# Projections in front of the down stage, softmax differences kept in PSUM, and layer norms finished by fours

## The chip, the cores and the metric

The kernel runs on one core of a Trainium2 chip. The metric is device time in microseconds, from the start to the end of one execution. An execution that was recorded by the hardware profiler gives the trace; its own time stands beside its span below.

## The reference

```python
xn = layernorm(x)                         # x: 2048 rows of 640
q, k, v = split(xn @ wqkv)                # 32 heads of 20
# row s attends to the 8 rows s, s-2, ..., s-14 (masked below row 0)
logits = einsum("bhsd,bhswd->bhsw", q, kg) * scale
o = einsum("bhsw,bhswd->bhsd", softmax(logits), vg)
h = (xn_B @ w_gate) * (xn_B @ w_up)       # 640 -> 1536; xn_B is the same xn
out = x + o @ wo + h @ w_down
```

Inputs and output are bf16.

## The kernel before

The 2048 rows are 16 tiles of 128 rows (t), four to a chunk (c = 0 to 3, `CH = 4`). For each chunk there are these stages:

- **Norm** (`ln`): for tiles 8 to 15 ScalarE takes the negative mean (`ln_mean`, L312) and the sum of squares (`ln_square`, L319), each with an accumulator output of one column; GpSimd makes three operations of one column per tile (L325, L327, L348); ScalarE applies the result to x in place (L355). Tiles 0 to 7 are done on VectorE.
- **Transposes** (`transposes`): from tile 4 on a transposing DMA on the SP queue (L395) writes xnT of the chunk, which has `XB` buffers.
- **Projections** (`project`, `proj`, L502 and L506): q, k and v, five groups of five matmuls each, each group evicted by ScalarE. `halo` copies the last 14 columns of the chunk before (L449). q, k and v have two buffers each, so chunk c + 2 writes over chunk c.
- **Products and logits** (`products`, `fold`, L565, L536, L541): VectorE multiplies q with shifted k and folds the result; `logits` (L587) sums over the head's dimensions with TensorE, into a bank of its own with two buffers.
- **Softmax** (`softmax`), twice per chunk (n = 0 to 7): maximum (L615), difference (L619), exp on ScalarE (L628), sum (L635), reciprocal (L638), scaling (L642) on VectorE; then the weights are stored to DRAM (aD, L648) and spread back over the partitions (aE, L654), both on the SP queue.
- **Weighted values** (`av`): per tile two products of v and aE (L681) and a tree of three additions (L691, L689) that ends in oT.
- **Gate and up** (`glu`): 24 groups of matmuls (L714), evicted by ScalarE (L719) into gs and us, and multiplied on VectorE into hT (L731); hT has 12 buffers, one chunk's.
- **Down** (`down`): per tile the matmuls of hT with wd (L780) and of oT with wo (L783), evicted to y (L795) and added to the output by a GpSimd DMA (L824); the last two tiles are added on VectorE (L791) and stored by SP.

Every operation is a `Step` with an engine, a cost, a part of the cost that occupies the engine (`occ`), and the steps it depends on. `Plan.order` simulates the engines with these costs, and at each time gives a free engine the ready step with the smallest latest time (`late`). The order that comes out is the program order of each engine's queue; on the chip each engine works its queue strictly in that order. All matmul groups but the logits are one chain in the order of declaration (`pe_main`), with a ring of six PSUM banks for their results. `margin` adds time, in the plan alone, after the steps that a step waits for. A transfer with `kb` ends in the plan by this rule, where its cost counts for `late` alone:

```python
if s.kb:
    s.end = queue[s.eng] = max(t0 + 2.0, queue.get(s.eng, 0.0)) + s.kb / 340
```

TensorE's chain is: projections of chunks 0 and 1, gate and up 0, down 0, projections 2, gate and up 1, down 1, projections 3, gate and up 2, down 2, gate and up 3, down 3. The norms of tiles 8 to 15 may start, by `LN_HOLD`, after hT products 2 to 5 of chunks 0 and 1.

Of the kernel before, what the change touches and what calls it, by code (L numbers as in the profile page):

```python
# [9 lines left out]
ACT = mybir.ActivationFunctionType  # L10
# [101 lines left out]
def kernel(  # L112
# [57 lines left out]
    def new(key, shape, dtype, tag, bufs, pool=None):  # L170
        t = (pool or sb).tile(shape, dtype, name=tag, tag=tag, bufs=bufs)
        T[key] = t
        return t
# [122 lines left out]
    def apply_in(t):  # L296
        XT[t] = inline("DVE", 0.443, ln_apply(t), [RS[t]], 0.4)

    LN_ACT = 8

    ST_ACT = (8, 9, 10, 11, 12, 13, 14, 15)

    LN_HOLD = ((0,2),(0,3),(0,4),(0,5),(1,2),(1,3),(1,4),(1,5))

    def held(at):
        return HT[at] if len(at) == 2 else R[at[0], at[1]][at[2]]

    def ln_mean(t):
        def fn():
            sq = new(("sq", t), [P, D], BF, "sq", 1)  # L310
            nm = new(("nm", t), [P, 1], F32, "nm", 6)
            nc.scalar.activation(sq[:], T["x", t][:], ACT.Identity, scale=-1.0 / D, accum_out=nm[:])  # L312
        return fn

    def ln_square(t):
        def fn():
            sq = new(("sq", t), [P, D], BF, "sq", 1)
            ss = new(("ss", t), [P, 1], F32, "ss", 4)
            nc.scalar.activation(sq[:], T["x", t][:], ACT.Square, bias=T["nm", t][:], accum_out=ss[:])  # L319
        return fn  # L320

    def ln_rstd_sq(t):
        def fn():
            ve = new(("ve", t), [P, 1], F32, "ve", 6)
            nc.gpsimd.tensor_scalar(ve[:], T["ss", t][:], scalar1=1.0 / D, scalar2=EPS, op0=ALU.mult, op1=ALU.add)  # L325
            rs = new(("rstd", t), [P, 1], F32, "rstd", 6)
            nc.gpsimd.tensor_tensor(rs[:], ve[:], mhalf[:], ALU.pow)  # L327
        return fn

    def ln(t):  # L330
        turn = [XT.get(t - (1 if t == CH else 2)), GL.get(t - 1)] if t < 2 * CH else []
        if t in ST_ACT:
            a = GL[t] = add("ACT", 0.95, ln_mean(t), [X[t], held(LN_HOLD[t - 2 * CH])], occ=0.87)
            a = add("ACT", 1.05, ln_square(t), [a], occ=0.97)
            b = RS[t] = add("POOL", 1.6, ln_rstd_sq(t), [a])
        else:
            a = add("DVE", 0.48, ln_stats(t, 0), [X[t], GL.get(t - 3), *turn], occ=0.395)
            a = add("DVE", 0.48, ln_stats(t, 1), [a], occ=0.395)
            a = GL[t] = add("DVE", 0.39, ln_aggr(t), [a], occ=0.3)
            b = RS[t] = add("POOL", 0.56, ln_rstd(t), [a])  # L340
        if t < LN_ACT:
            XT[t] = add("DVE", 0.443, ln_apply(t), [b], occ=0.35)
            return

        if t in ST_ACT:
            def shift():
                ns = new(("ns", t), [P, 1], F32, "ns", 6)
                nc.gpsimd.tensor_tensor(ns[:], T["nm", t][:], T["rstd", t][:], ALU.mult)  # L348
        else:
          def shift():  # L350
              ns = new(("ns", t), [P, 1], F32, "ns", 6)
              nc.gpsimd.tensor_scalar(ns[:], T["mv", t][:, 0:1], scalar1=T["rstd", t][:], scalar2=-1.0, op0=ALU.mult, op1=ALU.mult)

        def apply():
            nc.scalar.activation(T["x", t][:], T["x", t][:], ACT.Identity, scale=T["rstd", t][:], bias=T["ns", t][:])  # L355

        b = add("POOL", 0.5, shift, [b])
        XT[t] = add("ACT", 0.95, apply, [b], occ=0.85)


    ring = []
# [8 lines left out]
        return main  # L370

    XDMA = 4
    EARLY = False
    XB = 3 if EARLY else 2
    GP = {}

# [200 lines left out]
    def logits(c, g):  # L577
        n = 2 * c + g

        def lg():  # L580
            l = new(("lps", n), [P, W, E], F32, "pl", 2, psum)
            parts = [summed(c, 2 * g + b) for b in range(2)]
            last = len(parts[0]) - 1
            for i in range(last + 1):
                for b in range(2):
                    for j in range(4):
                        nc.tensor.matmul(l[H * j : H * (j + 1), 4 * b : 4 * b + 4, :], lhsT=Ek[:],  # L587
                                         rhs=parts[b][i][:, :, E * j : E * (j + 1)],
                                         start=(i == 0 and b == 0), stop=(i == last), tile_position=(0, H * j), skip_group_check=True)

        alone = not (g and c in PAIRED)
        took = 0.022 + 0.2195 * (len(LEFT) if c == 0 else 1) + (0.19 if alone else 0.0)
        LL[n] = add("PE", took + 0.13, lg, [FO[2 * n], FO[2 * n + 1], FO[4 * c + 3] if c in PAIRED else None, LL.get(n - 1), DD.get(n - 2), CE], occ=took)
        LL[n].urgent = True
        LL[n].margin = (0.9 if c == 0 else 3) if alone else 0.0

# [6 lines left out]
    def softmax(c, hf):  # L603
        n = 2 * c + hf

        def small(op, occ, deps):
            return add("DVE", occ + 0.083, op, deps, occ=occ)

        def mask():
            ps = T["lps", n]  # L610
            nc.vector.tensor_tensor(ps[0:H, :, 0:HALO], ps[0:H, :, 0:HALO], negm[0:H], ALU.add)

        def top():
            m = new(("m", n), [P, E], F32, "m", 1)
            nc.vector.tensor_reduce(m[:], T["lps", n][:].rearrange("p w s -> p s w"), AX.X, ALU.max)  # L615

        def sub():
            d = new(("d", n), [P, W, E], F32, "d", 1)
            nc.vector.tensor_tensor(d[:], T["lps", n][:], T["m", n][:, None, :].to_broadcast([P, W, E]), ALU.subtract)  # L619

        a = LL[n]
        if n == 0:
            a = small(mask, 0.2, [a, CM])
        a = small(top, 0.6, [a])
        DD[n] = small(sub, 0.609, [a, AA.get(n - 1)])

        def ex():
            nc.scalar.activation(T["d", n][:], T["d", n][:], ACT.Exp, scale=scale)  # L628

        e = add("ACT", 0.635, ex, [DD[n]], occ=0.54)  # L630
        e.margin = 0.8

        def total():
            s = new(("s", n), [P, E], F32, "s", 1)
            nc.vector.tensor_reduce(s[:], T["d", n][:].rearrange("p w s -> p s w"), AX.X, ALU.add)  # L635

        def rec():
            nc.vector.reciprocal(T["s", n][:], T["s", n][:])  # L638

        def scaled():  # L640
            a = new(("a", n), [P, W, E], BF, "a", 1)
            nc.vector.tensor_tensor(a[:], T["d", n][:], T["s", n][:, None, :].to_broadcast([P, W, E]), ALU.mult)  # L642

        AA[n] = small(scaled, 0.609, [small(rec, 0.47, [small(total, 0.6, [e])]), AS.get(n - 1)])

        def store():
            aD = new(("aD", n), [H, 4, W * E], BF, "aD", 2, dram)
            nc.sync.dma_start(out=aD[:].rearrange("h e f -> e h f"), in_=T["a", n][:].rearrange("p w s -> p (w s)"))  # L648

        def spread():  # L650
            ae = new(("aE", n), [P, 4, W, E], BF, "aE", 2)
            src = T["aD", n][:]
            src = bass.AP(tensor=src.tensor, offset=src.offset, ap=[[4 * W * E, H], [0, JL], [1, 4 * W * E]])
            nc.sync.dma_start(out=ae[:], in_=src)  # L654

        AS[n] = add("SP", 2.4, store, [AA[n], AE.get(n - 2)], occ=0.5, kb=128)
        AE[n] = add("SP", 3.5, spread, [AS[n], AM.get(2 * n - 3)], occ=0.5, kb=512)

    AS = {}
    ONE = True  # L660

# [6 lines left out]
    def av(t):  # L668
# [25 lines left out]
        w = LL[1] if t < 2 else O16.get(t - 2)  # L694
        a = add("DVE", 1.48, mul(0), [AE[n], w, *R[2, c]], occ=1.40, after=[O16.get(t - 1) if ONE else AM.get(t - 1)])
        a = AM[t] = add("DVE", 1.48, mul(1), [AE[n]], occ=1.40, after=[a])
        b = add("DVE", 1.485, tree(4), [a], occ=1.4)
        b = add("DVE", 0.82, tree(2), [b], occ=0.74)
        O16[t] = OE[t] = add("DVE", 0.49, tree(1), [b, DT.get(t - 4)], occ=0.41)

# [179 lines left out]
    proj(0, 1)  # L880
    proj(0, 2)

    def between(c, work):
        for q in range(CH):
            work(q)
            if c < NCH:
                ln(c * CH + q)
                transposes(c * CH + q)

    def attention(c):  # L890
        prodlog(c)
        if c == 0:
# [16 lines left out]
    for c in range(NCH):  # L909
        attention(c)  # L910
        glu(c)
        if c == 0:
            GS[0] = CM
            seed(0)
        for n in range(1, NCH):
            if SEED_AT[n][0] == c:
                seed(n)
        if EARLY:
            if c + 2 < NCH:
                for t in range((c + 2) * CH, (c + 3) * CH):  # L920
                    ln(t)
                    transposes(t)
                project(c + 2)
            for q in range(CH):
                down(c * CH + q)
        else:
            between(c + 2, lambda q: down(c * CH + q))
            if c + 2 < NCH:
                project(c + 2)

    for s in plan.order():
        s.fn()
# [30 lines left out]
```

## Time and profile before

| | us |
|---|---|
| median of 3 runs (260.49 to 261.25) | 261.0 |
| profiled execution, its own time | 260.88 |
| its span, first to last instruction | 259.2 |
| TensorE busy | 252.5 |
| VectorE busy | 228.6 |
| ScalarE busy | 128.8 |
| GpSimd busy | 47.9 |
| mean granted TensorE clock | 0.998 |

In the lines of the profile PE is TensorE, PEld its weight loads, DVE VectorE, ACT ScalarE, POOL GpSimd, SPq the SP queue. A line of a group has its line in the code, engine, operation, output and input, shape and count; behind the bar its busy time in us and the mean of one in ns; behind the second bar the engine's idle time just before these instructions and what ended it. A line of a timeline has the start and the duration in us, and in brackets the idle time before it.

### The profile page before, as it was taken

How to read it: one execution, taken by the hardware profiler on the slowest of the kernel's cores; microseconds unless marked ns; L12 is line 12 of the kernel's file. 1: busy time of each engine (PE TensorE's matmuls, PEld its weight loads, DVE VectorE, ACT ScalarE, POOL GpSimd, SP SyncE). 2: the span in 40 equal slices, each digit the busy share in tenths (PEclk: the TensorE clock that was granted, in tenths of full speed). 3: DMA queues.
4: the chain of work that ended last, by engine and by line, in shares of the span. 5: the costliest groups of instructions: out<-in, count | busy, mean ns of one | idle time of the engine just before them, and what ended most of it. 6: DMA issues, size and time to landing. Idle time of an engine off the chain costs nothing.

```text
span 259.2 us, 3845 instructions
## 1 busy us (share of the span) xinstructions
PE 252.5 (97%) x1493; PEld 140.2 (54%) x1493; DVE 228.6 (88%) x299; ACT 128.8 (50%) x251; POOL 47.9 (18%) x77
## 2 busy tenths in 40 slices
PE   7999999999999999999999999999999999999795
PEld 2955554444677554444476655444466744445562
DVE  5769999999999898999999967989999976999911
ACT  2756555699721365699931354555522242752100
POOL 2520000036641100036931200000302110000110
PEclk9999999999999999999999999999999999999999
DMA  7998996102274303015085241020112451020221
GB/s 223 333 206 236 397 374 229 58 3 101 57 147 43 34 6 97 0 23 182 3 183 73 25 85 41 16 88 0 51 52 25 41 75 64 0 101 3 25 25 53
DMA packets 19970, 24.49 MB, mean 94 GB/s; under 512 B 9104, under 2 KB 17296, under 8 KB 19888
## 3 DMA queue, kind: packets, MB, share of 16 engines
q1 hardware_dynamic: 16608, 17.70, 22.3%
q0 software_dynamic: 2384, 5.41, 12.8%
q10 hardware_dynamic: 960, 1.15, 1.2%
q8 instruction: 11, 0.18, 0.3%
q14 instruction: 7, 0.06, 0.1%
HBM read 18.61 MB, written 5.96 MB: 95 GB/s over the span
## 4 chain that ended last, share of the span: by engine, by line
DVE 41%; PE 39%; DMA 17%; issue 1%; ACT 0%; SPq 0%
PE ps L502 12%; PE ps L714 10%; DVE av L681 9%; PE ps L780 9%; DMA aE<-aD 9%; DVE pw L565 8%; DMA aD<-a 8%; DVE av L691 6%; DVE pw L536 4%; PE ps L783 4%; DVE hT L731 3%; PE ps L476 2%; DVE s L635 2%; PE ps L243 2%; DVE d L619 2%; DVE a L642 2%
## 5 line engine op out<-in xcount | busy, mean ns | idle before, releaser
L780 PE MATMUL ps<-wd,hT 128*128 128x320 bf16 (+2 forms) x384 | 57.8, 299 | 2.0 <-DVE hT L731 2.0
L714 PE MATMUL ps<-xnT,wg 128*128 128x512 bf16 x240 | 59.7, 379 | 0.0
L714 PE MATMUL ps<-xnT,wu 128*128 128x512 bf16 x240 | 59.6, 379 | 0.0
L681 DVE TENSOR_TENSOR av<-v,aE 128x2560 bf16<-128x2560 bf16 x32 | 47.1, 1486 | 10.2 <-DMA aE<-aD 10.2
L780 PEld LDWEIGHTS <-hT 128*128 128x128 bf16 x384 | 36.9, 98 | 18.6 <-DVE hT L731 2.6
L565 DVE TENSOR_TENSOR pw<-q,k 128x2560 bf16<-128x2560 bf16 x28 | 40.6, 1485 | 1.5 <-ACT k L506 1.5
L714 PEld LDWEIGHTS <-wu 128*128 128x128 bf16 x240 | 23.4, 98 | 28.3 <-issue 0.2
L714 PEld LDWEIGHTS <-wg 128*128 128x128 bf16 x240 | 23.3, 98 | 28.0 <-issue 0.4
L691 DVE TENSOR_TENSOR av<-av 128x2560 bf16<-128x2560 bf16 (+1 forms) x32 | 36.9, 1153 | 0.3
L719 ACT CAST gs<-ps 128x512 bf16<-128x512 f32 x48 | 28.1, 586 | 15.9 <-PE ps L714 15.8
L795 ACT COPY y<-ps 128x320 f32<-128x320 f32 x28 | 11.5, 427 | 49.0 <-PE ps L783 34.5
L719 ACT CAST us<-ps 128x512 bf16<-128x512 f32 x48 | 28.1, 584 | 13.8 <-PE ps L714 13.7
L824 POOL DMA_DIRECT2D out_dram<-y x14 | 12.2, 870 | 80.8 <-ACT y L795 78.3
L783 PE MATMUL ps<-wo,oT 128*128 128x320 bf16 (+2 forms) x160 | 27.0, 299 | 0.0
L536 DVE TENSOR_TENSOR pw<-pw 128x2048 bf16<-128x2048 bf16 (+1 forms) x28 | 25.1, 951 | 0.0
L502 PE MATMUL ps<-xnT,wk 128*128 128x512 bf16 x100 | 22.6, 380 | 0.0
L502 PE MATMUL ps<-xnT,wv 128*128 128x512 bf16 x100 | 22.2, 379 | 0.0
L731 DVE TENSOR_TENSOR hT<-gs,us 128x512 bf16<-128x512 bf16 x48 | 20.0, 417 | 0.4 <-ACT us L719 0.4
L325 POOL TENSOR_SCALAR ve<-ss 128x1 f32<-128x1 f32 x8 | 7.6, 952 | 66.1 <-ACT sq L319 65.7
L783 PEld LDWEIGHTS <-oT 128*128 128x128 bf16 x160 | 15.5, 98 | 6.3
L502 PEld LDWEIGHTS <-wv 128*128 128x128 bf16 x100 | 11.7, 117 | 9.8
L506 ACT CAST k<-ps 128x512 bf16<-128x512 f32 x20 | 11.7, 586 | 10.5 <-PE ps L502 10.5
(69 smaller groups left out, 224.0 us busy)
## 6 DMA issues: line engine op xcount, KB each, us to landing
aE<-aD SPq DMA_DIRECT2D x8, 512.0 KB, 3.6
out_dram<-y POOLq DMA_DIRECT2D x14, 160.0 KB, 3.7
out_dram<-in_A_x_dram POOLq DMA_DIRECT2D x3, 640.0 KB, 5.0
wg<-in_B_w_gate_dram SPq DMA_DIRECT2D x1, 1920.0 KB
wu<-in_B_w_up_dram SPq DMA_DIRECT2D x1, 1920.0 KB, 12.7
wd<-in_B_w_down_dram SPq DMA_DIRECT2D x1, 1920.0 KB
x<-in_A_x_dram SPq DMA_DIRECT2D x11, 160.0 KB, 6.1
aD<-a SPq DMA_DIRECT2D x8, 128.0 KB
```

The lines of the kernel that those rows point to most:

```text
L502: nc.tensor.matmul(T[key][:, 0:n], lhsT=lhs(r, i, j), rhs=T["xnT", c][:, i, lo : lo + n], start=(i == 0), stop=(i == KT - 1))
L506: nc.scalar.copy(where(r, c, j, j + 1, lo, n)[:, 0, :], T[key][:, 0:n])
L536: nc.vector.tensor_tensor(w[:, :, lo:hi, :], w[:, :, lo:hi, :], w[:, :, a:b, :], ALU.add)
L565: nc.vector.tensor_tensor(o, qh, kh, ALU.mult)
L681: nc.vector.tensor_tensor(o, v, w, ALU.mult)
L691: nc.vector.tensor_tensor(v[:, 0:k], v[:, 0:k], v[:, k : 2 * k], ALU.add)
L714: nc.tensor.matmul(ps[:], lhsT=(wu if r else wg)[:, i, f * P : (f + 1) * P], rhs=T["xnT", c][:, i, :], start=(i == 0), stop=(i == KT - 1))
L719: nc.scalar.copy(s[:], T[key][:])
L731: nc.vector.tensor_tensor(h[:], T["gs", c, f][:], T["us", c, f][:], ALU.mult)
L780: nc.tensor.matmul(ps, lhsT=T["hT", c, f][:, q * P : (q + 1) * P], rhs=wd[:, f, sl], start=(f == 0), stop=(f == FT - 1 and not wo_part))
L783: nc.tensor.matmul(ps, lhsT=T["oT", t][:, g, :], rhs=wo[:, g, sl], start=False, stop=(g == KT - 1 and f1 == FT))
L824: nc.gpsimd.dma_start(out=out_flat[t * P : (t + 1) * P, :], in_=T["y", t][:], accum_op=ALU.add)
```

## The change

- For chunks 2 and 3 the norms, transposes and projections are declared in front of the down stage of chunk 0 and 1 (`EARLY = True`), so TensorE's chain becomes: gate and up 0, projections 2, down 0, gate and up 1, projections 3, down 1, and on as before. xnT has three buffers instead of two.
- `ln_chunk` takes the place of `ln` for tiles 8 to 15. The means and sums of squares of four tiles go to four columns of one tile each; after the fourth, GpSimd makes three operations on four columns; then the four applies follow. `LN_HOLD` lets the norms of tiles 8 to 11 start after evictions of k and v of chunk 1, and those of 12 to 15 after the last hT product of chunk 0.
- The difference of the softmax is written over the logits in their PSUM bank, and exp, sum and scaling work there. The bank is free for logits n + 2 after the scaling instead of the difference.
- Costs in the plan: the store 3.3 instead of 2.4, the spread 3.9 instead of 3.5, the mask 0.18 instead of 0.2. `BY_DMA` is empty, so the tree of additions stays on VectorE.

```diff
-    LN_HOLD = ((0,2),(0,3),(0,4),(0,5),(1,2),(1,3),(1,4),(1,5))
+    LN_HOLD = ((1,1,0),(2,1,0),(2,1,2),(2,1,4),(0,11),(0,11),(0,11),(0,11))
...
+    def ln_finish(c):
+        def fn():
+            n4 = [P, CH]
+            ve = new(("ve4", c), n4, F32, "ve4", 2)
+            nc.gpsimd.tensor_scalar(ve[:], T["ss", c][:], scalar1=1.0 / D, scalar2=EPS, op0=ALU.mult, op1=ALU.add)
+            rs = new(("rs4", c), n4, F32, "rs4", 2)
+            nc.gpsimd.tensor_tensor(rs[:], ve[:], mhalf[:].to_broadcast(n4), ALU.pow)
+            ns = new(("ns4", c), n4, F32, "ns4", 2)
+            nc.gpsimd.tensor_tensor(ns[:], T["nm", c][:], rs[:], ALU.mult)
+        return fn
...
+    def ln_chunk(c):
+        ends = []
+        for q in range(CH):
+            t = c * CH + q
...
+            a = add("ACT", 0.95, mean, [X[t], held(LN_HOLD[t - 2 * CH])], occ=0.87, after=[ends[-1] if ends else None])
+            ends.append(add("ACT", 1.05, square, [a], occ=0.97))
+        b = add("POOL", 2.6, ln_finish(c), ends)
+        b.margin = 5.0
+        for q in range(CH):
+            t = c * CH + q
...
+            XT[t] = add("ACT", 0.95, apply, [b], occ=0.85, after=[XT[t - 1]])
+            transposes(t)
...
-    EARLY = False
+    EARLY = True
     XB = 3 if EARLY else 2
...
-        LL[n] = add("PE", took + 0.13, lg, [FO[2 * n], FO[2 * n + 1], FO[4 * c + 3] if c in PAIRED else None, LL.get(n - 1), DD.get(n - 2), CE], occ=took)
+        LL[n] = add("PE", took + 0.13, lg, [FO[2 * n], FO[2 * n + 1], FO[4 * c + 3] if c in PAIRED else None, LL.get(n - 1), AA.get(n - 2), CE], occ=took)
...
         def sub():
-            d = new(("d", n), [P, W, E], F32, "d", 1)
-            nc.vector.tensor_tensor(d[:], T["lps", n][:], T["m", n][:, None, :].to_broadcast([P, W, E]), ALU.subtract)
+            d = T["d", n] = T["lps", n]
+            nc.vector.tensor_tensor(d[:], d[:], T["m", n][:, None, :].to_broadcast([P, W, E]), ALU.subtract)
...
-            a = small(mask, 0.2, [a, CM])
+            a = small(mask, 0.18, [a, CM])
...
-        AS[n] = add("SP", 2.4, store, [AA[n], AE.get(n - 2)], occ=0.5, kb=128)
-        AE[n] = add("SP", 3.5, spread, [AS[n], AM.get(2 * n - 3)], occ=0.5, kb=512)
-
+        AS[n] = add("SP", 3.3, store, [AA[n], AE.get(n - 2)], occ=0.5, kb=128)
+        AE[n] = add("SP", 3.9, spread, [AS[n], AM.get(2 * n - 3)], occ=0.5, kb=512)
+
...
-        if EARLY:
-            if c + 2 < NCH:
-                for t in range((c + 2) * CH, (c + 3) * CH):
-                    ln(t)
-                    transposes(t)
-                project(c + 2)
-            for q in range(CH):
-                down(c * CH + q)
-        else:
-            between(c + 2, lambda q: down(c * CH + q))
-            if c + 2 < NCH:
-                project(c + 2)
+        if c + 2 < NCH:
+            ln_chunk(c + 2)
+        if EARLY and c + 2 < NCH:
+            project(c + 2)
+        for q in range(CH):
+            down(c * CH + q)
+        if not EARLY and c + 2 < NCH:
+            project(c + 2)
```

More of the change, by code (lines that the diff above doesn't have):

```diff
@@ L297, in apply_in @@
         XT[t] = inline("DVE", 0.443, ln_apply(t), [RS[t]], 0.4)
-    LN_ACT = 8
-    ST_ACT = (8, 9, 10, 11, 12, 13, 14, 15)
-    LN_HOLD = ((0,2),(0,3),(0,4),(0,5),(1,2),(1,3),(1,4),(1,5))
+    LN_HOLD = ((1,1,0),(2,1,0),(2,1,2),(2,1,4),(0,11),(0,11),(0,11),(0,11))
     def held(at):
         return HT[at] if len(at) == 2 else R[at[0], at[1]][at[2]]
-    def ln_mean(t):
+    def ln_finish(c):
         def fn():
-            sq = new(("sq", t), [P, D], BF, "sq", 1)
-            nm = new(("nm", t), [P, 1], F32, "nm", 6)
-            nc.scalar.activation(sq[:], T["x", t][:], ACT.Identity, scale=-1.0 / D, accum_out=nm[:])
-        return fn
@@ L315, in ln_square @@
[L315 to L328, printed above, removed]
+            n4 = [P, CH]
@@ new lines, in fn, with mean, square, apply @@
+            ve = new(("ve4", c), n4, F32, "ve4", 2)
[4 more added lines that the diff above has]
+            nc.gpsimd.tensor_tensor(ns[:], T["nm", c][:], rs[:], ALU.mult)
+        return fn
+    def ln_chunk(c):
+        ends = []
+        for q in range(CH):
+            t = c * CH + q
+            def mean(t=t, q=q):
+                if q == 0:
+                    new(("nm", c), [P, CH], F32, "nm4", 2)
+                    new(("ss", c), [P, CH], F32, "ss4", 2)
+                sq = new(("sq", t), [P, D], BF, "sq", 1)
+                nc.scalar.activation(sq[:], T["x", t][:], ACT.Identity, scale=-1.0 / D, accum_out=T["nm", c][:, q : q + 1])
+            def square(t=t, q=q):
+                sq = new(("sq", t), [P, D], BF, "sq", 1)
+                nc.scalar.activation(sq[:], T["x", t][:], ACT.Square, bias=T["nm", c][:, q : q + 1], accum_out=T["ss", c][:, q : q + 1])
+            a = add("ACT", 0.95, mean, [X[t], held(LN_HOLD[t - 2 * CH])], occ=0.87, after=[ends[-1] if ends else None])
[4 more added lines that the diff above has]
+            t = c * CH + q
+            def apply(t=t, q=q):
+                nc.scalar.activation(T["x", t][:], T["x", t][:], ACT.Identity, scale=T["rs4", c][:, q : q + 1], bias=T["ns4", c][:, q : q + 1])
+            XT[t] = add("ACT", 0.95, apply, [b], occ=0.85, after=[XT[t - 1]])
+            transposes(t)
@@ L330, in ln @@
     def ln(t):
         turn = [XT.get(t - (1 if t == CH else 2)), GL.get(t - 1)] if t < 2 * CH else []
[L332 to L335, printed above, removed]
-        else:
[L337 to L358, printed above, removed]
+        a = add("DVE", 0.48, ln_stats(t, 0), [X[t], GL.get(t - 3), *turn], occ=0.395)
+        a = add("DVE", 0.48, ln_stats(t, 1), [a], occ=0.395)
+        a = GL[t] = add("DVE", 0.39, ln_aggr(t), [a], occ=0.3)
+        b = RS[t] = add("POOL", 0.56, ln_rstd(t), [a])
@@ L361 @@
+        XT[t] = add("DVE", 0.443, ln_apply(t), [b], occ=0.35)
     ring = []
@@ L654, in spread @@
             nc.sync.dma_start(out=ae[:], in_=src)
-        AS[n] = add("SP", 2.4, store, [AA[n], AE.get(n - 2)], occ=0.5, kb=128)
-        AE[n] = add("SP", 3.5, spread, [AS[n], AM.get(2 * n - 3)], occ=0.5, kb=512)
+        AS[n] = add("SP", 3.3, store, [AA[n], AE.get(n - 2)], occ=0.5, kb=128)
+        AE[n] = add("SP", 3.9, spread, [AS[n], AM.get(2 * n - 3)], occ=0.5, kb=512)
+    BY_DMA = ()
     AS = {}
@@ L696, in av, with tree_dma @@
         a = AM[t] = add("DVE", 1.48, mul(1), [AE[n]], occ=1.40, after=[a])
-        b = add("DVE", 1.485, tree(4), [a], occ=1.4)
+        def tree_dma(k):
+            def fn():
+                v = T["av", t]
+                nc.gpsimd.dma_start(out=v[:, k : k + 2], in_=v[:, k + 4 : k + 6], accum_op=ALU.add)
+            return fn
+        if t in BY_DMA:
+            b = add("POOL", 4.5, tree_dma(0), [a], occ=0.9)
+            b = add("POOL", 4.8, tree_dma(2), [a], occ=1.15, after=[b])
+        else:
+            b = add("DVE", 1.485, tree(4), [a], occ=1.4)
         b = add("DVE", 0.82, tree(2), [b], occ=0.74)
@@ L881 @@
     proj(0, 2)
-    def between(c, work):
-        for q in range(CH):
[L885 to L888, printed above, removed]
     def attention(c):
@@ L917 @@
                 seed(n)
-        if EARLY:
-            if c + 2 < NCH:
-                for t in range((c + 2) * CH, (c + 3) * CH):
-                    ln(t)
-                    transposes(t)
-                project(c + 2)
-            for q in range(CH):
-                down(c * CH + q)
-        else:
-            between(c + 2, lambda q: down(c * CH + q))
-            if c + 2 < NCH:
-                project(c + 2)
+        if c + 2 < NCH:
[6 more added lines that the diff above has]
+            project(c + 2)
     for s in plan.order():
```

## The prediction

> **What bounds the kernel now.** I read the page first, then the groups by shape, then the timelines of TensorE, VectorE and the SP queue.
>
> From the page, the engines and one group:
>
> ```profile
> PE 252.5 (97%) x1493; PEld 140.2 (54%) x1493; DVE 228.6 (88%) x299; ACT 128.8 (50%) x251; POOL 47.9 (18%) x77
> ...
> L780 PE MATMUL ps<-wd,hT 128*128 128x320 bf16 (+2 forms) x384 | 57.8, 299 | 2.0 <-DVE hT L731 2.0
> ```
>
> TensorE is busy 97% of 259.2 us and is at its pace: in the timeline a projection's 25 matmuls of 512 columns start 5.39 us before the next one's, 0.216 us each, at granted clock 0.998, and this pace holds in the gate and up stages too. What it does not use is 1.3 us at the start, 0.4 in the first tile, 3.1 after its last matmul (one VectorE add and the last store), and 2.0 us in the last down projection. Only the 2.0 can be had by moving work. The timeline of TensorE places them:
>
> ```profile
> 235.10 1.39 PE L780 MATMUL ps<-wd,hT 128*128 128x320 bf16 x9
> 236.90 0.31 PE L780 MATMUL ps<-wd,hT 128*128 128x320 bf16 x1 [0.41 <-DVE hT L731]
> ...
> 241.63 2.21 PE L780 MATMUL ps<-wd,hT 128*128 128x320 bf16 x15 [1.57 <-DVE hT L731]
> ```
>
> TensorE waits for the hT products of the last chunk, which VectorE gives too late. The timeline of VectorE has them, and the holes that made it late:
>
> ```profile
> 156.97 2.90 DVE L681 TENSOR_TENSOR av<-v,aE 128x2560 bf16<-128x2560 bf16 x2 [3.45 <-DMA aE<-aD]
> ...
> 173.03 1.49 DVE L681 TENSOR_TENSOR av<-v,aE 128x2560 bf16<-128x2560 bf16 x1 [0.91 <-DMA aE<-aD]
> ...
> 216.31 2.89 DVE L681 TENSOR_TENSOR av<-v,aE 128x2560 bf16<-128x2560 bf16 x2 [4.15 <-DMA aE<-aD]
> ...
> 239.75 1.48 DVE L681 TENSOR_TENSOR av<-v,aE 128x2560 bf16<-128x2560 bf16 x1
> 241.16 0.42 DVE L731 TENSOR_TENSOR hT<-gs,us 128x512 bf16<-128x512 bf16 x1
> ```
>
> The inputs of the last hT were there at 235.9 (us eviction 235.30 plus 0.59). It ran at 241.16: VectorE's order is fixed by the planner, and VectorE came to this place late. It works without a break from 233.3 to 245.9. So the bound is TensorE, with VectorE 2.0 us too late at one place.
>
> **The change part by part.** All against the profiled execution, 260.88 us (span 259.2 and 1.7 around it); the median is 261.0, 0.1 above.
>
> *Softmax differences in the logits' bank.* Count and order stay; d is read and written in PSUM. The groups by shape:
>
> ```profile
> L635 DVE TENSOR_REDUCE s<-d 128x64 f32<-128x512 f32 x8 | 8.3, 1034 | 0.1
> L619 DVE TENSOR_TENSOR d<-pl,m 128x512 f32<-128x512 f32 x8 | 5.5, 691 | 0.2
> L642 DVE TENSOR_TENSOR a<-d,s 128x512 bf16<-128x512 f32 x8 | 5.5, 687 | 0.2
> L615 DVE TENSOR_REDUCE m<-pl 128x64 f32<-128x512 f32 x8 | 5.5, 686 | 0.7 <-PE pl L587 0.7
> ```
>
> The sum over the window (L635) and the maximum (L615) have the same pattern, 512 elements read in steps of 64; the sum reads SBUF and takes 1.034, the maximum reads PSUM and takes 0.686. Either the memory or the operation makes the 0.348. I take the memory, the nearest row for a reduction out of PSUM: 8 x 0.348 = 2.8 us less on VectorE. Other end: it stays 1.034, nothing saved. The subtraction (PSUM source, 0.691) and the scaling (SBUF source, 0.687) cost the same now, so they stay; for a PSUM destination no row of this size exists, the mask in PSUM (112 elements, 0.262) is 0.145 above its 112 cycles at 0.96 GHz as L619 is 0.158 above its 512, so plus or minus 0.02 each. The exp is on ScalarE, 0.632 now, 0.586 for a PSUM source of the same size: 0 to 0.05 less per softmax, off the bound.
>
> [...]
>
> *Projections in front of down.* Same matmuls, other order, so TensorE's floor does not move: project(2) would run at 66.9 to 83.1 (3 x 5.4), down 0 (18.5) to 101.6, and gate/up 1 begins at about 102 as now (102.48). Likewise project(3) 128.4 to 144.6, then down 1 to 163.5. What each needs: v of chunk 2 overwrites v of chunk 0 (two buffers), last read by L681 until 73.9, first needed free at 78.8; down 0 needs oT of chunk 0, last one at 76.8, before it starts; down 1 needs oT 7, at 132.2, before 144.6. hT of chunk 1 reuses hT of chunk 0 after down 0 at 101.6, before its first inputs at 104. The first oT of chunk 1 (111.7) needs oT 0 read, then at about 88. All covered; the tightest is v with 5 us.
>
> The gain is that q and k of chunk 3 are evicted by 139.8 instead of 159.3, so that VectorE has products for the hole of 3.45 at 153.5. The planner sees a smaller hole: its two transfers take 2.38 + 3.51 = 5.9 us, while 150.00 to 156.97 is 7.0; so 1.1 us stays, and some 2.3 us are filled. The hole of 0.91 stays: the products were ready in front of it already and the planner didn't take them. The 4.15 stays, as no products are left then. Ends: 0 to 4.4.
>
> *Norms.* The same 24 ScalarE passes (mean 0.744, square 0.832, each with an accumulator read of 0.2, apply 0.921), but earlier: the four tiles of chunk 2 in the evictions of k and v of chunk 1 (30.6 to 41.4) instead of from 49.3. Their x landed before 31 (issued 21.5 to 23.0, 7.7 us at most). ScalarE has 0.49 idle per 1.08 us there; four tiles of about 1.8 delay an eviction by 2 us at most, and six PSUM banks of 1.08 us cover 6.5. The last square ends near 43.5. GpSimd then makes three operations for four columns: a set of three now takes 0.952 + 0.830 + 0.911 = 2.7; ends 2.7 and four times that, 10.8; I take 2.7, since columns of one element can be little but the fixed part. The planner places the applies 7.6 us after the squares; at 10.8 ScalarE's queue would stand 3.2 us with gate/up evictions behind it, inside the 6.5. Applies then end between 57 and 60.
>
> Transposes move with them on the SP queue, past a store and a spread:
>
> ```profile
> 57.78 0.56 SPq L648 DMA_DIRECT2D aD<-a  x1
> 61.06 0.54 SPq L654 DMA_DIRECT2D aE<-aD  x1
> 67.15 5.22 SPq L395 DMA_TRANSPOSE xnT<-x  x4
> ```
>
> Four issues of 1.24 and 3.3 to land: done by 61 to 65, and TensorE needs them at 66.9. The third xnT buffer removes the wait for gate/up 0. The x loads 13 to 15 on GpSimd's queue follow them and may meet the spread at 61 (3.6 us in the median, 4.9 the slowest): at most 1.3 us for VectorE, once, early. Norms of chunk 3 run from 68 on, 60 us before they are needed. Cost 0.
>
> *Changed costs for store and spread, mask:* they only move priorities; a little earlier softmax. 0.
>
> *The sum.* The last hT must come 2.0 us earlier. A hole that the planner fills does not do that by itself: it also plans more work in front of that hT, as its place follows from the inputs at 236.3. What helps is less lateness against the plan. The plan has 0.6 for the sum where 0.95 passes until the next instruction, and VectorE has waited for TensorE only once since 45 us (0.7), so the 2.8 us arrive nearly in full: the last hT ends at 241.58 - 2.8 = 238.8, needed at 239.6 (241.58 less 1.98). Stall gone with 0.8 to spare: 260.88 - 2.0 = 258.9, on the median's scale 259.0. More than that the change can't give.
>
> **Rivals.**
> - *The sum stays at 1.03, or the order keeps the last hT late.* For: only one row speaks for PSUM, and the spread of chunk 3 (211.37 to 216.29, against 3.5 planned) delays VectorE after the plan as before. Against: either saving alone is over 2.0. Then 0 to 1.3 us of the 2.0 are won: 259.6 to 261.0.
> - *Slower: TensorE stands at 66.9 for the transposes of chunk 2.* If all four queue behind the spread at 61.06, they issue from 61.6 to 66.6 and land at 69.9: a wait of 3.0. Everything behind moves by that, and the stall at the end is gone, since VectorE doesn't move: 259.0 + 3.0 = 262.0. It decides at the last apply: after about 62 us it happens. For: the whole chain took from 49.3 to 75 before, 26 us, and from 37 (second tile) this is 63. Against: GpSimd's part shrinks and no wait for gate/up 0 is left.
> - *A new wait of TensorE in its own queue for logits.* Logits 6 and 7 stand 1.6 and 1.7 us behind their last fold now (197.6 to 199.18, 211.5 to 213.17); if the new order makes VectorE later by more, each waits a microsecond: 260 to 262.
>
> **How the numbers follow.** Stall gone: 0.52, 258.5 to 259.5 (the runs of before spread 0.76 us). Hardly anything or a part: 0.24, of it 0.15 faster and 0.09 within the bound. Transposes: 0.14, of it 0.11 slower. Logits and the like: 0.10, of it 0.02 faster, 0.02 same, 0.06 slower. The bound of 0.3% is 0.8 us, about what a measurement of this kernel can tell from no change. Faster 0.69, same 0.14, slower 0.17. Low 258.5, as the floor stands; high 261.5 leaves out the full transposes case and the worst of the last.
>
> **What would show it.** Right: L635 at 0.69; the idle time of L780 behind hT under 0.3; no idle time of L502 at 66.9; the hole before L681 near 153 down to about 1; the last hT before 239.6. Wrong: L635 at 1.03, an idle time of TensorE at 66.9 behind a transpose, of L587 behind pw, or of an eviction behind ns4; or a time under 258, which would mean that TensorE's work itself got shorter.

## The result

The changed kernel takes 262.5 us in the median (six runs, 261.66 to 263.48), the kernel before 260.96 (six runs, 260.49 to 261.25). The ratio is 1.0064, 95% interval 1.0041 to 1.0087. It is slower by 1.5 us, where 259.0 was forecast and 261.5 was the end of the range. Two of the six runs, 263.13 and 263.48 us, show a granted clock of 0.993; the other four have a median of 262.3, still 1.3 above. The profiled execution took 262.27 us with a span of 260.6, 1.4 above the span of before, at a granted clock of 1.0.

The page of the changed kernel, its engines and the two groups that hold the waits in question:

```profile
PE 252.9 (97%) x1493; PEld 140.2 (54%) x1493; DVE 225.5 (87%) x299; ACT 128.4 (49%) x251; POOL 32.2 (12%) x59
...
L783 PE MATMUL ps<-wd,hT 128*128 128x320 bf16 (+2 forms) x384 | 58.1, 299 | 2.8 <-DVE hT L734 2.7
...
L674 DVE TENSOR_TENSOR av<-v,aE 128x2560 bf16<-128x2560 bf16 x32 | 47.0, 1487 | 14.1 <-DMA aE<-aD 14.1
```

The last of these lines in the kernel before:

```profile
L681 DVE TENSOR_TENSOR av<-v,aE 128x2560 bf16<-128x2560 bf16 x32 | 47.1, 1486 | 10.2 <-DMA aE<-aD 10.2
```

VectorE has 3.1 us less work (228.6 before), yet the wait of TensorE for the last hT products grew from 2.0 to 2.7, and VectorE's idle time behind aE, the softmax weights that come back from DRAM, grew from 10.2 to 14.1. The saving became waiting. The timeline of TensorE has the stall at two places of the last down stage again, 1.95 and 0.72 us, where it was 0.41 and 1.57 before:

```profile
235.90 1.39 PE L783 MATMUL ps<-wd,hT 128*128 128x320 bf16 x9
239.24 0.31 PE L783 MATMUL ps<-wd,hT 128*128 128x320 bf16 x1 [1.95 <-DVE hT L734]
...
243.11 2.21 PE L783 MATMUL ps<-wd,hT 128*128 128x320 bf16 x15 [0.72 <-DVE hT L734]
```

The last down stage, down 3, begins at 235.90 instead of 235.10. So 0.8 us was lost ahead of it, and 0.7 is added stall; together they are the 1.4 us of the span, within the rounding. The timeline of VectorE, the holes of chunks 2 and 3:

```profile
156.64 2.89 DVE L674 TENSOR_TENSOR av<-v,aE 128x2560 bf16<-128x2560 bf16 x2 [0.46 <-DMA aE<-aD]
...
174.31 1.49 DVE L674 TENSOR_TENSOR av<-v,aE 128x2560 bf16<-128x2560 bf16 x1 [2.88 <-DMA aE<-aD]
...
216.14 2.90 DVE L674 TENSOR_TENSOR av<-v,aE 128x2560 bf16<-128x2560 bf16 x2 [6.37 <-DMA aE<-aD]
```

The first hole shrank from 3.45 to 0.46, as products of chunk 3 fill it. The other two grew, 0.91 to 2.88 and 4.15 to 6.37. VectorE finished the scaling of softmax 6 at 206.2 instead of 208.0, and aE still landed at 216.1, where it landed at 216.3 before.

Why it did shows in two timelines of the changed kernel, the SP queue with the store of the weights (aD) and their spread (aE), and GpSimd's queue with the output writes of the down stage:

```profile
165.33 0.55 SPq L640 DMA_DIRECT2D aD<-a  x1
170.64 0.54 SPq L646 DMA_DIRECT2D aE<-aD  x1
206.26 0.55 SPq L640 DMA_DIRECT2D aD<-a  x1
211.23 0.54 SPq L646 DMA_DIRECT2D aE<-aD  x1
```

```profile
165.03 0.86 POOL L827 DMA_DIRECT2D out_dram<-y  x1 [3.76 <-ACT y L798]
...
203.10 0.88 POOL L827 DMA_DIRECT2D out_dram<-y  x1 [6.31 <-ACT y L798]
205.51 0.86 POOL L827 DMA_DIRECT2D out_dram<-y  x1 [1.53 <-ACT y L798]
```

The spread is issued when the store has landed (in the kernel before SP waits for the landing in front of all eight spreads, 22.4 us in sum). For softmax 5 that is 5.31 us, for softmax 6 4.97 us after the store, where both took 3.3 before:

```profile
166.02 0.55 SPq L648 DMA_DIRECT2D aD<-a  x1
169.31 0.54 SPq L654 DMA_DIRECT2D aE<-aD  x1
208.05 0.54 SPq L648 DMA_DIRECT2D aD<-a  x1
211.37 0.54 SPq L654 DMA_DIRECT2D aE<-aD  x1
```

Each time an output write of 160 KB had been issued just before the store, 0.30 and 0.75 us ahead. The write at 165.03 is that of tile 7: down 1 runs behind projections 3 now, so its writes come at 150.8 to 165.0 instead of 134.0 to 148.2.

The spread of softmax 6 is long too, 4.9 us from issue to landing, but it took 4.9 before as well; in both kernels the write of tile 11 is issued shortly ahead of it, at 210.13 and 209.68. What takes longer than before is the store.

### The profile page after: what moved, and what is told of

Its sections match the earlier page's. It is cut to its first block, busy times and chain, and to the rows that moved or that the text cites. A ratio compares the mean times of both kernels' runs of the same rounds, so it can differ in the third digit from the quotient of the medians.

```text
span 260.6 us, 3827 instructions
## 1 busy us (share of the span) xinstructions
PE 252.9 (97%) x1493; PEld 140.2 (54%) x1493; DVE 225.5 (87%) x299; ACT 128.4 (49%) x251; POOL 32.2 (12%) x59
## 4 chain that ended last, share of the span: by engine, by line
PE 77%; DVE 15%; DMA 7%; issue 1%; ACT 0%; SPq 0%
PE ps L717 29%; PE ps L494 23%; PE ps L783 14%; PE ps L786 6%; DMA aE<-aD 3%; DVE pw L557 3%; DMA aD<-a 3%; DVE av L674 3%; PE ps L468 2%; DVE pw L528 2%; PE ps L243 2%; DVE av L684 2%; DVE hT L734 2%; PE pl L579 1%; DVE pl L611 1%
## 5 line engine op out<-in xcount | busy, mean ns | idle before, releaser
L674 DVE TENSOR_TENSOR av<-v,aE 128x2560 bf16<-128x2560 bf16 x32 | 47.0, 1487 | 14.1 <-DMA aE<-aD 14.1
L494 PE MATMUL ps<-xnT,wk 128*128 128x512 bf16 x100 | 22.4, 379 | 0.0
L494 PE MATMUL ps<-xnT,wv 128*128 128x512 bf16 x100 | 22.4, 379 | 0.0
L494 PEld LDWEIGHTS <-wk 128*128 128x128 bf16 x100 | 11.6, 117 | 9.7 <-issue 0.2
L494 PE MATMUL ps<-xnT,wq 128*128 128x512 bf16 x75 | 16.7, 379 | 0.0
```

The lines of the kernel that those rows point to most:

```text
L494: nc.tensor.matmul(T[key][:, 0:n], lhsT=lhs(r, i, j), rhs=T["xnT", c][:, i, lo : lo + n], start=(i == 0), stop=(i == KT - 1))
L674: nc.vector.tensor_tensor(o, v, w, ALU.mult)
```

## The experiments

The theory formed from these rows: an output write that starts just ahead of the store of the weights stretches it; the change moved down 1's writes onto softmax 5, and the delay from there put softmax 6 behind a write of chunk 2. Its rivals: the order of VectorE, fixed by a planner that is too optimistic, makes the last hT late by itself; or the norms or the PSUM differences cost something of their own. The ratios below are against the kernel before, measured beside each kernel.

**PSUM differences alone** (e1), on the kernel before:

```diff
+            d = T["d", n] = T["lps", n]
+            nc.vector.tensor_tensor(d[:], d[:], T["m", n][:, None, :].to_broadcast([P, W, E]), ALU.subtract)
...
+        LL[n] = add("PE", took + 0.13, lg, [FO[2 * n], FO[2 * n + 1], FO[4 * c + 3] if c in PAIRED else None, LL.get(n - 1), AA.get(n - 2), CE], occ=took)
```

> The kernel before with one part of the change: the softmax differences stay in the logits' PSUM bank. Theory A (the sum out of PSUM is cheaper, and the saving is lost later because the weights' store and spread of the last chunk run beside the output writes): L635 about 0.69, 2.8 us of VectorE saved, the chain from scaling to aE of softmax 6 grows above the 8.3 us of before or keeps its place, stall of TensorE at the last hT 1 to 2 us, time 260 to 261. Theory B (the step of the prediction, lateness alone): the saving arrives at the last hT, stall under 0.5, time 259.0.

Measured: ratio 0.9998 (0.9981 to 1.0014), median 261.14. The sum takes 0.684 us, so 2.8 us less, and nothing arrives. GpSimd's and SP's timelines of this kernel:

```profile
148.29 0.86 POOL L824 DMA_DIRECT2D out_dram<-y  x1 [4.20 <-ACT y L795]
```

```profile
148.75 0.54 SPq L648 DMA_DIRECT2D aD<-a  x1
154.00 0.55 SPq L654 DMA_DIRECT2D aE<-aD  x1
```

VectorE came 1.25 us earlier to softmax 4, and so the store fell 0.46 us behind the write of tile 7, which in the kernel before (148.22) lay 1.8 us ahead of it. The store took 5.25 instead of 3.4 us and VectorE's hole grew from 3.45 to 5.50; the wait for the weights of softmax 7 grew by another 0.5 (0.44 to 0.95). The last hT starts at 241.02 (241.16 before), and the stall stays at 1.8. All engines work in the same order as in the kernel before, so theory B, lateness alone, is out.

**Projections behind down again** (e2): the changed kernel with `EARLY = False`.

> The changed kernel with EARLY = False: projections behind down again, two xnT buffers; norms by fours and PSUM differences stay. Theory A (down 1 and down 2 moved their output writes into the time of softmax 4 to 6, which stretched store and spread from 7.0 to 9 or 10 us): store plus spread of softmax 5 back to about 7 us, time 259.5 to 261. Rival (the norms or the new costs of the plan did it): time stays at 262 to 263.

Measured: 0.9996 (0.9981 to 1.0010), median 261.04. Stores of softmax 5 and 6 are back at 3.27 and 3.30 us. So the loss comes with the moved projections and down stages. It is no gain either: the stall at the last hT products is gone, but TensorE now waits 1.4 us for an eviction of q near 94 and 0.3 for an hT at 135.

**Differences in SBUF** (e3): the changed kernel with the old `sub`, and `DD.get(n - 2)` in `LL[n]`.

> The changed kernel with the differences in SBUF as before. If the sum's 0.35 us per softmax counts at the end: 264 to 265 (2.8 us on VectorE back). If the end is set by store and spread and by the order, with slack in between: 262.5 to 263.5.

Measured: 1.0083 (1.0061 to 1.0105), median 263.18. This lies in the second range: the 2.8 us of VectorE are worth at most 0.7 here. The store of softmax 6 falls 1.09 us behind a write (205.45 to 206.54) and takes 4.59.

**Without the output writes of chunks 1 and 2** (e4), of chunk 1 (e5), of chunk 2 (e6); the other queues keep their order. The edit of e4; e5 has `(1,)` and e6 `(2,)` in its place:

```diff
-            else:
+            elif c not in (1, 2):
                 nc.gpsimd.dma_start(out=out_flat[t * P : (t + 1) * P, :], in_=T["y", t][:], accum_op=ALU.add)
```

> The changed kernel without the eight output writes of chunks 1 and 2 (those rows of the output are left out); every other queue has the same order. Theory A (these writes stretch the weights' store and spread): the chain from scaling to aE of softmax 5 and 6 falls from 9.1 and 10.0 to about 7.0, av of tile 12 starts near 213.2 instead of 216.1, the stall at the last hT falls from 2.7 under 0.5, time 259.5 to 260.3. Rival (stretched by something else, such as the store waiting on SP or the fixed order of VectorE): within 0.5 us of 262.5.

> The changed kernel without the four output writes of chunk 1 (those rows are left out). Theory (each write that overlaps a store or spread stretches it, and the two chunks hit different softmaxes): chain from scaling to aE of softmax 5 falls from 9.1 to about 7.1, that of softmax 6 stays 8.5 to 10; VectorE reaches the scaling of softmax 6 near 204.3 instead of 206.2; a part of the gain: 260.5 to 262. Rival (chunk 2's writes alone matter): 262.5.

> The changed kernel without the four output writes of chunk 2 (those rows are left out). Theory: chain of softmax 6 falls from 10.0 to about 7.2, av of tile 12 starts near 213.3 instead of 216.1, the stall at the last hT falls from 2.7 to 0.3 or less, 259.5 to 260.5. Rival (the delay of softmax 5 carries through): 261.5 to 262.5.

Measured: e4 0.9911 (0.9892 to 0.9930), median 258.83; e5 0.9912 (0.9893 to 0.9931), 258.81; e6 0.9945 (0.9926 to 0.9965), 259.76. The group of the down matmuls in e4:

```profile
L783 PE MATMUL ps<-wd,hT 128*128 128x320 bf16 (+2 forms) x384 | 57.6, 299 | 0.0
```

No stall is left, and the time is the floor of the prediction, 258.9, below the 259.5 to 260.3 that I had expected for e4. The expectation of e5 was too small as well: I had expected only a part of the gain. Here are SP's and GpSimd's timelines of e5 at softmax 6:

```profile
204.54 0.55 SPq L640 DMA_DIRECT2D aD<-a  x1
207.92 0.54 SPq L646 DMA_DIRECT2D aE<-aD  x1
```

```profile
205.17 0.85 POOL L827 DMA_DIRECT2D out_dram<-y  x1 [2.91 <-ACT y L798]
```

Without chunk 1's writes the scaling of softmax 6 ends at 204.5, the store starts 0.6 us ahead of tile 10's write instead of behind it and takes 3.38; the second collision follows from the first. In e6 the first remains in part (write 165.23, store 166.68, 3.94 us) and the stall is 0.5.

**Control: the kernel before without the same writes** (e7).

> Control: the kernel before without the eight output writes of chunks 1 and 2 (those rows are left out). Theory (before, the writes met the spread of softmax 6 alone, 4.9 instead of 3.6 us): aE of softmax 6 lands 1.3 earlier, stall 2.0 to about 0.7: 259.5 to 260.3, so that the changed kernel without writes (258.8) is faster than this one. Rival (the writes cost both kernels the same): 258.5 to 259.3.

Measured: 0.9953 (0.9937 to 0.9969), median 260.08, stall 1.0. The spread of softmax 6 takes 3.6 us here instead of 4.9, so in the kernel before the write of tile 11 had stretched it. The writes cost the kernel before 1.2 us and the changed one 3.7 (262.5 to 258.83; 4.0 by the two ratios), and without them the changed kernel is faster by 1.25: the change's gain is there.

**Holding writes back instead of leaving them out** (e9 tile 7, e8 tiles 9 to 11, e10 all four). A small copy on GpSimd reads one element of aE, and the held writes stand behind it in the queue; the orders of TensorE, VectorE and ScalarE are those of the changed kernel:

```diff
+        def wait():
+            g = new(("gate", "w", n), [P, 1], BF, "gate", 1)
+            nc.gpsimd.tensor_copy(g[0:1, 0:1], T["aE", n][0:1, 0, 0, 0:1])
+
+        w = add("POOL", 0.2, wait, [AE[n]])
+        for t, (st, evs) in HELD.items():
+            if HOLD[t] == n:
+                OB[t] = add("POOL", 4.5, st, [*evs, CP[t // CH], w], occ=0.5)
```

In e8 and e10 y has three buffers, and mv, ve and rstd have four instead of six to make room.

> The changed kernel with nothing left out: the output writes of tiles 9, 10 and 11 wait on GpSimd's queue for one element of aE of softmax 6, three y buffers instead of two; the orders of TensorE, VectorE and ScalarE are the same. Theory: as without the writes of chunk 2, if the held writes don't meet softmax 7: chain of softmax 6 near 7.2 to 7.7 (tile 8's write may overlap), 259.7 to 261, faster than both kernels. Rival (the writes only move and hurt softmax 7 instead): 261.5 to 263.

> The changed kernel with nothing left out and one edit: the output write of tile 7, the last of chunk 1, waits on GpSimd's queue for one element of aE of softmax 5. Theory (that write starts 0.3 us ahead of the store of softmax 5 and stretches it from 3.3 to 5.3 us; VectorE, then 1.9 us late, brings the store of softmax 6 right behind the write of tile 10): chain of softmax 5 near 7.2, scaling of softmax 6 ends near 204.5, av of tile 12 starts near 212.3, no stall at the last hT, 258.6 to 259.4. Rival (chunk 2's writes stretch softmax 6 all the same): 260 to 261.5.

> The changed kernel with tile 7's write behind aE of softmax 5 and those of tiles 9 to 11 behind aE of softmax 6, three y buffers. Theory: TensorE's floor, 258.6 to 259.2, no better than holding tile 7 alone. Rival (the held writes hurt softmax 7): 260 or more.

Measured: e8 0.9947 (0.9927 to 0.9967), median 259.98; e9 0.9927 (0.9897 to 0.9956), 259.11; e10 0.9899 (0.9871 to 0.9926), 258.84. The SP queue, and the down group, of e9:

```profile
166.00 0.55 SPq L640 DMA_DIRECT2D aD<-a  x1
169.32 0.54 SPq L646 DMA_DIRECT2D aE<-aD  x1
204.87 0.55 SPq L640 DMA_DIRECT2D aD<-a  x1
208.19 0.54 SPq L646 DMA_DIRECT2D aE<-aD  x1
```

```profile
L794 PE MATMUL ps<-wd,hT 128*128 128x320 bf16 (+2 forms) x384 | 57.6, 299 | 0.0
```

One write moved out of the way of softmax 5 turns 262.5 into 259.1: both stores are back at 3.32 us and the stall is gone. It is a narrow escape at softmax 6, though: the write of tile 10 is issued at 205.11, 0.24 us behind the store. Nine of the twelve runs of e9 took 258.48 to 259.36 and three 261.00 to 261.88, all at a granted clock of 1.0; those of e10, which holds these writes as well, took 258.62 to 259.16. That the store fell behind the write in the three long runs would fit, but none of them was profiled. e8 shows the other half: the store of softmax 5 still takes 4.72 us, that of softmax 6 only 3.41, and a stall of 0.6 is left. e10 is the version to keep: 1.0% under the kernel before.

**Tile 7 held, differences in SBUF** (e12).

> Tile 7's write held as above, and the softmax differences in SBUF as before. If the 0.35 us per sum reach the end once the writes are out of the way: last hT about 2 us later than with PSUM, stall 1 to 2 us, 260 to 261. If they are absorbed: as with PSUM, 258.6 to 259.4.

Measured: 1.0052 (1.0029 to 1.0075), median 262.85, worse than expected. GpSimd's and SP's timelines:

```profile
205.32 0.86 POOL L838 DMA_DIRECT2D out_dram<-y  x1 [2.06 <-ACT y L809]
```

```profile
205.94 0.55 SPq L640 DMA_DIRECT2D aD<-a  x1
211.13 0.54 SPq L646 DMA_DIRECT2D aE<-aD  x1
```

VectorE is 1.1 us later at softmax 6 than in e9, the store slips behind the write of tile 10 and takes 5.19 us, and TensorE stands for 2.29 us at the last hT products. Then a lower granted clock is added, 0.993 over this execution; in e3 a wait of the same 2.29 us left it at 1.0. The timeline of TensorE has it right behind the stall, in the ten matmuls that took 1.52 us in the changed kernel:

```profile
239.29 0.31 PE L794 MATMUL ps<-wd,hT 128*128 128x320 bf16 x1 [2.29 <-DVE hT L734]
...
240.12 2.51 PE L794 MATMUL ps<-wd,hT 128*128 128x320 bf16 x10
```

The next matmuls start 2.30 us after these ten and not 1.36, and the five that follow (1.54 us instead of 0.84) take 0.66 more as well; so the clock costs this execution about 1.6 us. Six of the twelve runs show 0.992 or 0.993; the other six have a median of 262.15. So 1.1 us of lateness became 3.0 us at full clock and 3.7 over all runs.

**Early projections alone** (e11): the kernel before with `EARLY = True`.

> The kernel before with EARLY = True alone: norms by single tiles, differences in SBUF, plan's costs as before. Theory (moving down 1 behind the projections brings its writes to softmax 5): write of tile 7 within 1 us ahead of the store of softmax 5 or 4, that store above 4.5 us, 262 to 264. Rival (the norms or PSUM are needed for the loss): 260.5 to 261.5.

Measured: 1.0588 (1.0531 to 1.0645), which stands on the three fastest of six runs, median 277.46; all six took 275.2 to 284.26, at granted clocks of 0.964 to 0.981. The expectation was far off. The timeline of TensorE:

```profile
71.13 7.28 PE L502 MATMUL ps<-xnT,wq 128*128 128x512 bf16 x25 [3.75 <-DMA xnT<-x]
...
143.39 7.29 PE L502 MATMUL ps<-xnT,wq 128*128 128x512 bf16 x25 [7.31 <-DMA xnT<-x]
```

With the old `LN_HOLD` the transposes come too late for projections that no longer stand behind down; TensorE waits 11.1 us for them. Behind each wait 25 matmuls take 7.28 or 7.29 us that take 5.56 in the changed kernel; the granted clock over the execution is 0.975. The early projections need the earlier norms. What the moved writes alone would have cost stays open here.

## Why the prediction was wrong, point by point

- *The sum out of PSUM*: right in size. L627 takes 0.684 us out of PSUM (0.69 expected) where L635 took 1.034 out of SBUF, the subtraction takes 0.699, the exp 0.587; VectorE's work fell by 3.1 us, 2.8 expected. So it was the memory and not the operation. The 0.96 in the prediction's account of the subtraction is a pace that the kernel before shows: the adds of L791 take 0.292, 0.492 and 0.692 us for 128, 320 and 512 columns, 0.96 columns per ns.
- *Norms*: right. GpSimd's three operations on four columns take 0.894 + 1.216 + 0.662 = 2.77 us (2.7 taken), the transposes of chunk 2 were issued from 54.7 to 60.6, and projections 2 began at 67.11 without a wait. The slower rival named there, TensorE standing for the transposes, did not come up in the changed kernel; e11 shows that it is real without this part.
- *Projections in front of down*: the timetable was right within 0.6 us (67.1, 83.3, 128.55, 145.2), and the hole of 3.45 shrank to 0.46 (1.1 expected; in e8 to e10 it is 1.4 to 1.8).
- *"The hole of 0.91 stays", "The 4.15 stays"*: **this is the step that failed.** They became 2.88 and 6.37. I moved the matmuls of down 1 to 144.6 to 163.5 and counted their inputs, but not the four output writes that they issue, which moved along to 150.8 to 165.0 and stand in the sum at nothing. In place of that nothing the runs showed 3.4 us: e9 holds back one of these writes, that of tile 7, and takes 259.11 instead of 262.5. Of the DMAs I had weighed the x loads against the spread of softmax 1, and nothing against softmax 4 to 7.
- *"So the 2.8 us arrive nearly in full"*: wrong for the same reason. The last hT ended at 243.1, where 238.8 was forecast. An earlier VectorE issues the store at another moment, and whether that store meets an output write decides more than the 2.8 us: e1 saved 2.8 and gained nothing, e12 was 1.1 late and lost 3.0 at full clock. (The prediction dates the inputs of the last hT at 235.9 and again at 236.3; the profile has 235.89, and the sum rests on neither.)
- *The floor, 258.9 and "more than that the change can't give"*: right; e4, e5 and e10 reach 258.8 with no stall.
- *Rivals*: none had this mechanism. The one that kept the last hT late came nearest, with the wrong reason (the sum or the order) and, at its worst, no gain. Neither of the two that forecast a loss came up: TensorE did not stand for the transposes of chunk 2, and none of its waits is at the logits.

Left open: the 0.8 us that TensorE lost before down 3. The profile shows 0.19 of it at a group of gate and up that waits for an eviction, while ScalarE's queue stood 4.91 us at the exp of softmax 7 for VectorE; the rest carries no named wait. In e9 and e10 down 3 begins at 235.15 and 235.26, so most of it goes with the lateness, but it was not tried by itself. The same kind of stand at the exp of softmax 6 (4.03 us) held back the evictions of down 2, which is why tile 9's write came only at 203.10, 2.4 us ahead of tile 10's instead of 5.05; this too was seen and not tried.

## What to carry to other kernels

When a stage is moved, list every DMA that it issues and lay it against each chain of DMAs that an engine waits for in the new neighbourhood; a store of 3.3 us on such a chain is worth more attention than the matmuls beside it. A saving on an engine that feeds such a chain shifts the chain in time, so what it is worth depends on what it meets there. Where a large write has slack, as that of tile 7 here (some 30 us until its y buffer is written again), holding it behind the landing of the chain costs one small instruction, 1.44 us on GpSimd in e9.

## What the runs showed of the hardware

A store of 128 KB on SP's queue takes 3.3 us until the spread that waits for it is issued, and up to 2.0 us more if an output write of 160 KB on GpSimd's queue was issued shortly ahead. The rows are of softmax 4 to 6 alone; at softmax 1 and 2 of the changed kernel transposes run beside the store.

| write ahead of store, us | store to spread, us | kernel, softmax |
|---|---|---|
| 0.30 | 5.31 | changed, 5 |
| 0.46 | 5.25 | e1, 4 |
| 0.62 | 5.19 | e12, 6 |
| 0.74 | 4.72 | e8, 5 |
| 0.75 | 4.97 | changed, 6 |
| 1.09 | 4.59 | e3, 6 |
| 1.45 | 3.94 | e6, 5 |
| 1.78 | 3.43 | before, 4 |
| 2.34 | 3.31 | e3, 5 |
| 2.99 | 3.32 | before, 6 |
| -0.07 (write behind) | 3.74 | e3, 4 |
| -0.10 (write behind) | 3.71 | e11, 5 |
| -0.24 (write behind) | 3.32 | e9, 6 |
| -0.63 (write behind) | 3.38 | e5, 6 |

Which of the two comes first decides most: a write 0.30 us ahead costs the store 2.0 us, one 0.07 or 0.10 behind costs it 0.4, and one 0.24 behind does no harm that can be seen. The writes show the other side. In the changed kernel those of tiles 7 and 10, issued 0.30 and 0.75 us ahead of a store, take 4.3 and 3.6 us from issue to landing, and those of tiles 5 and 6, which meet no store, 3.5 and 3.6. So two queues are no protection (5.31 against 3.32 us), and of the pair 0.30 us apart the later transfer bears most: the store takes 2.0 us longer, the write 0.7 or 0.8.

The spread of 512 KB can be stretched too. At softmax 6 it takes 4.4 to 4.9 us where the write of tile 11 was issued 1.1 to 1.8 us ahead of it (before, changed, e1, e3, e12), and 3.6 to 4.0 in e6 to e10, where none was; but e4's took 4.54 with no write near it.

A stall of TensorE can cost more than its length. Behind waits of 3.75 and 7.31 us in e11 25 matmuls took 7.28 and 7.29 us instead of 5.56, and the granted clock of that execution is 0.975; behind 2.29 us in e12 ten took 2.51 instead of 1.52, at 0.993. But behind 2.29 us in e3 and 1.95 in the changed kernel ten took 1.52 and the clock is 1.0, and half of e12's runs show no loss of clock. No run here settles when it comes.
